# A fused attention and feed-forward kernel: GpSimd and the transfers in program order, one batch turned by TensorE, two kinds of work given to VectorE

## The chip, the cores and the metric

The kernel runs on one core of one Trainium2 chip. The metric is device microseconds of one execution. The engines are named as in the profile: PE is TensorE's matmul stream, PEld its weight load, DVE is VectorE, ACT ScalarE, POOL GpSimd, SP SyncE, whose queue issues most transfers. A line such as L657 is a line of the kernel that ran. PSUM is the memory that TensorE writes to, in banks; the kernel sets three of them aside for attention, as the pool "at".

## The reference, cut to what matters

```python
# q, k, v: (8 batches, 8 heads, 576 tokens, 64), float32; g_norm: (64,)
kv  = einsum('bhsd,bhse->bhde', k, v)
o   = einsum('bhsd,bhde->bhse', q, kv)
rms = sqrt(mean(o * o, axis=-1, keepdims=True) + 1e-06)
x   = (o / rms * g_norm)          # -> 4608 rows of 512
h   = (x @ w1) * (x @ w2) @ w3    # w1, w2: 512 x 1024; w3: 1024 x 1024
out = h @ w_out                   # w_out: 1024 x 512
```

All is float32. The weights arrive in 64 bits and are converted on the chip.

## The kernel before

It folds w3 and w_out into one matrix first (0 to 84 us, the "fold"). Then come nine groups of 512 tokens, which I call T0 to T8: 512 rows of each of the eight batches, and the eight left-over blocks of 64 rows as a ninth. A group is four quarters of "gates" (x w1 times x w2, L569) and a projection (times the folded matrix, L841), both in forms with seven products in place of eight, whose sums VectorE makes. A quarter of gates has four result blocks, finished in the order c12, c22, c11, c21. T0 still converts weights and prepares the folded matrix's sums. T0 to T6 each prepare the next batch's attention besides, in eight steps, two to a quarter. The order of execution is T0 to T6, then the left rows, then the last batch. In the changed kernel the same lines are L615 (gates) and L886 (projection).

A batch's q, and its normalized output, must be turned (transposed) before TensorE can use them. This is done by GpSimd and a transfer:

```python
def turn_by_dma(srcs, apart, turned, dsts):            # (cut)
    nc.gpsimd.tensor_copy(to, words(src) ...)          # L284, L286: split fp32 into two uint16 planes
    yield
    nc.sync.dma_start_transpose(out=turned, in_=apart) # L288
    yield
    nc.gpsimd.tensor_copy(words(dst), src)             # L298: put the planes together
```

The steps of a batch, in the kernel before:

```python
fs[1] += [(a.begin_kv, 2, 3), (a.finish, 0)]     # finish: product and norm of one half
fs[2].append((a.begin_q, 2, 3))                  # turn the other half's q
fs[3].append((a.turn_two, 0))                    # turn the normalized half: this is x
...
fs[5].append((a.finish, 1))
fs[6].append((batch(b + 1).begin_q, 0, 1))       # the NEXT batch's q
fs[6].append((a.turn_two, 1))                    # x, second half
if b % 2:                                        # odd batches: the left rows of two batches
    fs[2].insert(0, (a.q_t_left,))
    fs[4].append((a.product_left,))
    fs[6].append((a.turn_left,))
```

The product takes two of the three "at" banks and its norm reads them:

```python
def product(h):
    o_ps = [bank(ps_at, "at") for _ in range(2)]
    ...                                          # 64 matmuls, L395 (L409 after)
    return norm(o_ps, ...)
def product_left():
    o_ps = [bank(ps_at, "at") for _ in range(2)]
    ...                                          # 32 matmuls, L413 (L427 after)
def norm(o_ps, dsts):
    ...                                          # square (ACT), reduce (DVE), sqrt (ACT), reciprocal (DVE)
    nc.vector.tensor_tensor(out=dsts[i], in0=o_ps[i] ..., in1=inv ..., op=ALU.mult)   # L373 (L387 after)
```

When x is there, VectorE makes the sums of the next group's x: `combine_x`, L611 (L657 after). The gates' own ends are the addition and the product of gates:

```python
nc.vector.tensor_add(c, one, two)                    # L707 (L753 after)
nc.vector.tensor_mul(dst, c[:, 0, :], c[:, 1, :])    # L708 (L754 after)
```

Only TensorE executes in program order (`manual_schedule(engines={PE})`). The order of the instructions on every other engine is set by a scheduler when the kernel is built. Each engine then works through its own list, and an instruction that waits holds up those behind it: in the prediction's lines of T3, VectorE stands 6.37 us at L611 with the gate product L708 behind it.

## Time and profile before

| | us |
|---|---|
| median of three runs | 842.67 (840.91 to 843.88) |
| span of the profiled execution | 840.2 |
| TensorE busy | 779.8 |
| TensorE idle | 60.4 |
| T0 | 110.1 |
| T1, T2, T3, T4, T5, T6 | 82.8, 85.4, 84.8, 85.0, 84.5, 77.5 |
| left rows; last batch with tail | 70.4; 75.6 |

A group begins with its first gate matmul on TensorE's timeline. The left rows show what a group costs with no attention beside it, 70.4 us. The prediction shows the lines of the page that carry this.

### The profile page before, as it was taken

The numbers are of one execution on the slowest core, as the hardware profiler recorded it, in microseconds if no ns is written. First come the engines' busy times: TensorE is split into PE (matmuls) and PEld (weight loads), VectorE is DVE, ScalarE is ACT, GpSimd is POOL, SyncE is SP. The second block draws the span as 40 slices with busy tenths as digits, with TensorE's granted clock in tenths as the row PEclk, the third lists the DMA queues.
The fourth block names the chain that finished last, engine by engine and source line by source line (L and its number), as shares of the span: only waits on it lengthen the run. The fifth ranks groups of instructions, "written<-read, shape, count | busy, mean of one in ns | idle before, by whom it ended". The sixth has DMA issues, their size and how long they took to land.

```text
span 840.2 us, 14371 instructions
## 1 busy us (share of the span) xinstructions
PE 779.8 (93%) x5747; PEld 674.4 (80%) x5747; DVE 537.0 (64%) x1050; ACT 245.7 (29%) x476; POOL 201.4 (24%) x176
## 2 busy tenths in 40 slices
PE   8999786979989998899889997999799999999997
PEld 6455675868879887898789877987798898899897
DVE  7958889923548655754485567554755983575366
ACT  6677431302221322122212221322123222222221
POOL 0016547671340135013301350033003300000000
PEclk9999996999999999899989998999899999999999
DMA  9997663488555747564646564656462263037005
GB/s 323 326 321 217 161 141 78 154 239 293 93 126 192 226 84 158 176 226 95 126 167 226 104 151 147 224 125 126 139 219 51 39 232 127 0 132 226 0 24 184
DMA packets 140166, 134.37 MB, mean 160 GB/s; under 512 B 84036, under 2 KB 128068, under 8 KB 140100
## 3 DMA queue, kind: packets, MB, share of 16 engines
q1 hardware_dynamic: 137648, 118.64, 50.7%
q10 hardware_dynamic: 2452, 14.81, 5.1%
q8 instruction: 45, 0.74, 0.4%
q14 instruction: 21, 0.17, 0.1%
HBM read 100.27 MB, written 16.38 MB: 139 GB/s over the span
## 4 chain that ended last, share of the span: by engine, by line
PE 63%; DMA 10%; DVE 9%; issue 8%; POOL 8%; SPq 1%; ACT 1%; POOLq 0%; DVEq 0%; ACTq 0%
PE mm L569 34%; PE mm L841 19%; PE mm L551 5%; DMA q_sb<-qT 3%; DMA xn<-xT 2%; DMA w3o_sb<-w3o_l 2%; POOL xT L284 1%; PE at L319 1%; POOL w_sb L167 1%; DVE ab L708 1%; PE at L395 1%; DMA w3o_l<-stage 1%; POOL qT L298 1%; DVE xc L611 1%; DVE c L707 1%
## 5 line engine op out<-in xcount | busy, mean ns | idle before, releaser
L569 PE MATMUL mm<-xT,w_sb 128*128 128x256 f32 x768 | 177.0, 380 | 0.0
L569 PEld LDWEIGHTS mm<-xT,w_sb 128*128 128x128 f32 x768 | 146.3, 191 | 20.1 <-issue 0.5
L569 PE MATMUL mm<-xc,ws 128*128 128x256 f32 x576 | 134.1, 386 | 6.1 <-ACT p L582 6.1
L569 PEld LDWEIGHTS mm<-xc,ws 128*128 128x128 f32 x576 | 111.3, 194 | 22.3 <-ACT p L582 6.9
L707 DVE TENSOR_TENSOR c<-mm,u 128x512 f32<-128x512 f32 x36 | 24.8, 689 | 128.0 <-PE mm L569 128.0
L582 ACT COPY u<-mm 128x512 f32<-128x512 f32 x74 | 43.3, 585 | 167.0 <-PE mm L569 137.2
L286 POOL COPY qT<-q_sb 128x1024 uint16<-128x1024 uint16 x28 | 30.9, 1127 | 242.1 <-PE at L395 209.0
L569 PE MATMUL mm<-xc,w_sb 128*128 128x256 f32 x288 | 71.5, 392 | 8.1 <-ACT u L582 8.1
L841 PE MATMUL mm<-w3o_sb,ab 128*128 128x128 f32 x336 | 48.4, 290 | 25.3 <-DVE ab L708 24.5
L582 ACT COPY p<-mm 128x512 f32<-128x512 f32 x74 | 43.1, 585 | 86.9 <-PE mm L569 77.8
L569 PEld LDWEIGHTS mm<-xc,w_sb 128*128 128x128 f32 x288 | 54.6, 194 | 16.8 <-ACT u L582 8.9
L841 PE MATMUL mm<-w3o_sb,raw 128*128 128x128 f32 x500 | 67.0, 288 | 0.4 <-DMA w3o_sb<-w3o_l 0.4
L841 PEld LDWEIGHTS mm<-w3o_sb,ab 128*128 128x128 f32 x336 | 44.6, 205 | 26.5 <-DVE ab L708 25.3
L841 PEld LDWEIGHTS mm<-w3o_sb,raw 128*128 128x128 f32 x500 | 63.6, 204 | 0.8 <-issue 0.6
L569 PE MATMUL mm<-xT,ws 128*128 128x256 f32 x256 | 62.3, 387 | 0.2 <-ACT p L582 0.2
L551 PE MATMUL mm<-chunks,ab 128*128 128x512 f32 x128 | 60.2, 601 | 0.6 <-ACT ab L543 0.6
L708 DVE TENSOR_TENSOR ab<-c 128x256 f32<-128x256 f32 x108 | 56.2, 520 | 2.9
L569 PEld LDWEIGHTS mm<-xT,ws 128*128 128x128 f32 x256 | 49.2, 194 | 7.7 <-ACT p L582 0.6
L167 POOL TENSOR_SCALAR w_sb<-w_sb,g_col 128x1024 f32<-128x1024 f32 x8 | 26.6, 3323 | 82.0 <-ACT kv_sb L330 46.8
L298 POOL COPY xT<-xn 128x1024 uint16<-128x1024 uint16 x28 | 34.1, 1246 | 49.8 <-DMA xn<-xT 49.8
L707 DVE TENSOR_TENSOR c<-p,u 128x512 f32<-128x512 f32 x36 | 27.0, 751 | 29.4 <-ACT u L582 29.1
L298 POOL COPY qT<-q_sb 128x1024 uint16<-128x1024 uint16 x28 | 34.0, 1225 | 31.2 <-DMA q_sb<-qT 31.1
(153 smaller groups left out, 1169.5 us busy)
## 6 DMA issues: line engine op xcount, KB each, us to landing
w3o_sb<-w3o_l SPq DMA_DIRECT2D x26, 896.0 KB, 4.8
raw<-in_moe_w_dram SPq DMA_DIRECT2D x31, 512.0 KB, 7.4
raw<-w3o_l SPq DMA_DIRECT2D x13, 896.0 KB, 4.7
w3o_sb<-w3o_l ACTq DMA_DIRECT2D x11, 896.0 KB, 4.6
k_sb<-in_k_dram SPq DMA_DIRECT2D x32, 256.0 KB, 4.7
v_sb<-in_v_dram SPq DMA_DIRECT2D x32, 256.0 KB, 4.8
q_sb<-in_q_dram SPq DMA_DIRECT2D x32, 256.0 KB, 2.9
out_dram<-raw SPq DMA_DIRECT2D x14, 512.0 KB, 6.1
```

Of the source, the lines that this page charges most:

```text
L167: nc.gpsimd.tensor_scalar(out=dst, in0=dst, scalar1=scale, scalar2=None, op0=ALU.mult)
L284: nc.gpsimd.tensor_copy(to, src.rearrange("p a n w -> p w a n"))
L286: nc.gpsimd.tensor_copy(to, words(src).rearrange("p n w -> p w n"))
L298: nc.gpsimd.tensor_copy(words(dst), src)
L319: nc.tensor.matmul(kv_ps[e * D:(e + 1) * D, r - rs[0], :], lhsT=k_sb[:, e, cols] if j < J else kl[:, 2 * r + e, :], rhs=v_sb[:, e, cols] i ...
L395: nc.tensor.matmul(o_ps[l][tokens, n * D:(n + 1) * D], lhsT=qT[r][rows, e, i, tokens], rhs=kv_b[rows, e, r, :], start=True, stop=True,)
L551: nc.tensor.matmul(sums_ps[half][m], lhsT=w3T[half, c][:, m, :], rhs=chunks[:, c, 1, :], start=(c == 0), stop=(c == KF - 1),)
L569: nc.tensor.matmul(ps[:, u, :], lhsT=lhsT(a_name, u, c), rhs=rhs(b_name, c),  start=(u == 0 and c == 0 and to is None), stop=(c == chunks ...
L582: nc.scalar.copy(t, ps)
L707: nc.vector.tensor_add(c, one, two)
L708: nc.vector.tensor_mul(dst, c[:, 0, :], c[:, 1, :])
L841: nc.tensor.matmul(to[:, i, :], lhsT=x[:, c, :], rhs=y[:, c, :], start=new and place // 4 not in seen, stop=(c == 1), skip_group_check=True,)
```

## The change

The intent is to free TensorE from waits for GpSimd. Four parts:

1. the scaling of the weights by g goes from GpSimd to VectorE;
2. in T0, batch 1's q and x are turned by TensorE with ScalarE copies;
3. the 28 subtractions for the folded matrix's sums go from GpSimd to VectorE, and from T0 into T1's steps;
4. GpSimd and SyncE follow the program's order, the program puts x ahead of q, the last copies of a turn come one step after its begin, and the left product of later odd batches moves from step 4 to step 5.

```diff
-            nc.gpsimd.tensor_scalar(out=dst, in0=dst, scalar1=scale, scalar2=None, op0=ALU.mult)
+            nc.vector.tensor_scalar(out=dst, in0=dst, scalar1=scale, scalar2=None, op0=ALU.mult)
 ...                                              # steps(b)
+        def turn(i, f, *args):                   # copies and transfer in step i, last copies in step i + 1
+            ...
         if b == 1:
+            fs[0] += [(a.begin_kv, 0, 1), (a.begin_q, 0, 1)]
         fs[1] += [(a.begin_kv, 2, 3), (a.finish, 0)]
-        fs[2].append((a.begin_q, 2, 3))
-        fs[3].append((a.turn_two, 0))
+        if b == 1:
+            fs[2] += [(a.q_t_left,), (a.begin_q, 2, 3)]
+            fs[3] += [(a.turn, 0), (a.turn, 1)]
+        else:
+            turn(2, a.x_by_dma, 0)
+            turn(2, a.q_two_by_dma, 2, 3)
+            if odd:
+                turn(3, a.q_left_by_dma)
         ...
         fs[5].append((a.finish, 1))
-        fs[6].append((batch(b + 1).begin_q, 0, 1))
-        fs[6].append((a.turn_two, 1))
-        if b % 2: ...                            # q left 2, product_left 4, turn_left 6
+        if odd:
+            fs[5 if b > 1 else 6].append((a.product_left,))
+        if b == 1:
+            fs[7] += [(a.turn, 2), (a.turn, 3), (a.turn_left,)]
+        else:
+            turn(6, a.x_by_dma, 1)
+            if odd:
+                turn(6, a.x_left_by_dma)
         if more:
+            turn(6 if b > 1 else 7, batch(b + 1).q_two_by_dma, 0, 1)
 ...                                              # prepare_b, now a generator run from T1's steps
-            nc.gpsimd.tensor_sub(t1, b12, b11)   # and three more
+            nc.vector.tensor_sub(t1, b12, b11)   # and three more
 ...
-    ctx.enter_context(tc.manual_schedule(engines={mybir.EngineType.PE}))
+    ctx.enter_context(tc.manual_schedule(
+        engines={mybir.EngineType.PE, mybir.EngineType.Pool, mybir.EngineType.SP}
+    ))
```

More of the change, by code (lines that the diff above doesn't have):

```diff
@@ L298, in turn_by_dma, with together @@
             nc.gpsimd.tensor_copy(words(dst), src)
+    def together(turns):
+        turns = list(turns)
+        while turns:
+            turns = [t for t in turns if next(t, turns) is None]
+            yield
     def attention(b):
@@ L346, in q_by_dma @@
             to = qT[r].rearrange("p e i t -> p (e i t)")
-            all_of(turn_by_dma([q_sb], to, q_sb, [to]))
+            return turn_by_dma([q_sb], to, q_sb, [to])
         st = {}
@@ L352, in q_t_left, with q_left_by_dma @@
             st["qT"] = work.tile([P, NP, P], FP32, name="qT_left", bufs=1)
+            qt_ps = bank(ps_at, "at").rearrange("p (r t) -> p r t", r=NP)
+            for r in range(NP):
+                nc.tensor.transpose(qt_ps[:, r, :], q_left[b // 2][:, 2 * r:2 * r + 2, :], ident)
+            nc.scalar.copy(st["qT"], qt_ps)
+        def q_left_by_dma():
+            st["qT"] = work.tile([P, NP, P], FP32, name="qT_left", bufs=1)
             src = q_left[b // 2].rearrange("p h d -> p (h d)")
             to = st["qT"].rearrange("p r t -> p (r t)")
-            all_of(turn_by_dma([src], to, src, [to]))
+            return turn_by_dma([src], to, src, [to])
         def norm(o_ps, dsts):
@@ L430, in turn, with x_by_dma @@
             nc.scalar.copy(dst, t_ps.rearrange("p (i j) t -> p i (j t)", i=2))
-        def turn_two(h):
+        def x_by_dma(h):
             xn, x = st[h].rearrange("p i l m d -> p (i l) (m d)"), xT[b][:, h]
@@ L437, in turn_two @@
             half = [slice(r * G, (r + 1) * G) for r in range(2)]
-            turns = [
+            return together(
                 turn_by_dma(
@@ L442, in turn_two, with x_left_of, x_left_by_dma @@
                 for r in range(2)
-            ]
-            for _ in range(2):
-                for t in turns:
-                    next(t)
-            for t in turns:
-                all_of(t)
-        def turn_left():
-            n = b // 2
-            x = x_left[:, :, n // 2, :, (n % 2) * P:(n % 2 + 1) * P]
-            xn = st["left"].rearrange("p r e d -> p (r e d)")
+            )
+        def x_left_of():
+            n = b // 2
+            return x_left[:, :, n // 2, :, (n % 2) * P:(n % 2 + 1) * P]
+        def turn_left():
+            t_ps = bank(ps_at, "at").rearrange("p (h r t) -> p h r t", h=2, t=P)
+            for r in range(NP):
+                nc.tensor.transpose(t_ps[:, r // 2, r % 2, :], st["left"][:, r], ident)
+            nc.scalar.copy(x_left_of(), t_ps)
+        def x_left_by_dma():
+            x, xn = x_left_of(), st["left"].rearrange("p r e d -> p (r e d)")
             apart = st["qT"].rearrange("p r t -> p (r t)")
-            all_of(turn_by_dma([xn], apart, xn, [x[:, h] for h in range(2)]))
+            return turn_by_dma([xn], apart, xn, [x[:, h] for h in range(2)])
         def load_ahead(names, r):
@@ L473, in begin_q, with q_two_by_dma, loads @@
             for r in rs:
-                q_by_dma(r)
+                q_t(r)
                 load_ahead("q", r)
+        def q_two_by_dma(*rs):
+            def loads():
+                yield
+                yield
+                for r in rs:
+                    load_ahead("q", r)
+            return together([*(q_by_dma(r) for r in rs), loads()])
         def begin(r):
@@ L480, in begin @@
             load_ahead("q", r)
-        first_done = []
-        def begin_first():
-            if not first_done:
-                first_done.append(begin_q(0, 1))
         def finish(h):
@@ L491, in attention @@
         return SimpleNamespace(**{f.__name__: f for f in (
-            start, begin_kv, begin_q, begin_first, begin, product, finish, turn, turn_two, q_t_left, product_left,
-            turn_left,
+            start, begin_kv, begin_q, begin, product, finish, turn, q_t_left, product_left, turn_left,
+            q_two_by_dma, q_left_by_dma, x_by_dma, x_left_by_dma,
         )})
@@ L508, in steps, with begin @@
         more = b + 1 < B
-        fs = [[] for _ in range(8)]
+        fs, ends = ([[] for _ in range(8)] for _ in range(2))
+        def turn(i, f, *args):
+            t = []
+            def begin():
+                t.append(f(*args))
+                next(t[0])
+                next(t[0])
+            fs[i].append((begin,))
+            if i + 1 < 8:
+                ends[i + 1].append((lambda: all_of(t[0]),))
+            else:
+                to_end.append((lambda: all_of(t[0]),))
+        ends[0] += to_end
+        to_end.clear()
+        odd = b % 2
         if b == 1:
-            fs[0].append((a.begin_kv, 0, 1))
+            fs[0] += [(a.begin_kv, 0, 1), (a.begin_q, 0, 1)]
         fs[1] += [(a.begin_kv, 2, 3), (a.finish, 0)]
-        fs[2].append((a.begin_q, 2, 3))
-        fs[3].append((a.turn_two, 0))
+        if b == 1:
[6 more added lines that the diff above has]
+                turn(3, a.q_left_by_dma)
         if more:
@@ L517, in steps @@
         fs[5].append((a.finish, 1))
-        if more:
-            fs[6].append((batch(b + 1).begin_q, 0, 1))
-        fs[6].append((a.turn_two, 1))
-        if b % 2:
-            fs[2].insert(0, (a.q_t_left,))
-            fs[4].append((a.product_left,))
-            fs[6].append((a.turn_left,))
-            if more:
-                fs[7].append((load_q_left, b + 1))
-        elif more:
-            fs[0].append((load_q_left, b + 1))
-        return iter([lambda s=s: [f(*args) for f, *args in s] for s in fs])
+        if odd:
+            fs[5 if b > 1 else 6].append((a.product_left,))
+        if b == 1:
+            fs[7] += [(a.turn, 2), (a.turn, 3), (a.turn_left,)]
+        else:
+            turn(6, a.x_by_dma, 1)
+            if odd:
+                turn(6, a.x_left_by_dma)
+        if more:
+            turn(6 if b > 1 else 7, batch(b + 1).q_two_by_dma, 0, 1)
+            fs[7 if odd else 0].append((load_q_left, b + 1))
+        return iter([lambda s=e + f: [f(*args) for f, *args in s] for e, f in zip(ends, fs)])
+    to_end = []
     w3T = {}
@@ L744, in b_blocks @@
         return [b[0, 0], t1, t2, b[1, 1], b[0, 1], b[1, 0], t4]
-    def stage_tile():
-        return late_pool.tile([P, 3, 2, P], FP32, name="stage")
     def prepare_b():
@@ L758, in prepare_b @@
             )
-            stage = stage_tile()
-            t1, t2, t4 = (stage[:, i] for i in range(3))
-            nc.gpsimd.tensor_sub(t1, b12, b11)
-            nc.gpsimd.tensor_sub(t2, b22, t1)
-            nc.gpsimd.tensor_sub(b12, b22, b12)
-            nc.gpsimd.tensor_sub(t4, b21, t2)
+            stage = o_sbs[n % 2].rearrange("p m n -> p (m n)")[:, 0:6 * P]
+            t1, t2, t4 = (t.rearrange("p (c n) -> p c n", n=P) for t in (
+                stage[:, i * 2 * P:(i + 1) * 2 * P] for i in range(3)
+            ))
+            nc.vector.tensor_sub(t1, b12, b11)
+            nc.vector.tensor_sub(t2, b22, t1)
+            nc.vector.tensor_sub(b12, b22, b12)
+            nc.vector.tensor_sub(t4, b21, t2)
             nc.sync.dma_start(
@@ L767, in prepare_b @@
             )
-            nc.sync.dma_start(
-                out=w3o_l2[n, :, 1024:PART], in_=stage.rearrange("p i c n -> p (i c n)")
-            )
+            nc.sync.dma_start(out=w3o_l2[n, :, 1024:PART], in_=stage)
+            yield
     loaded_b = []
@@ L942 @@
     w3o_l2 = dram.tile([8, P, PART], FP32, name="w3o_l2")
-    ctx.enter_context(tc.manual_schedule(engines={mybir.EngineType.PE}))
+    ctx.enter_context(tc.manual_schedule(
+        engines={mybir.EngineType.PE, mybir.EngineType.Pool, mybir.EngineType.SP}
+    ))
     fold = fold_cm.__enter__()
@@ L1040, in between @@
             next(pieces, lambda: None)()
+            if T == 1:
+                for _ in range(2):
+                    next(preparing, None)
+                if len(loaded_b) == 0 and next(preparing, 0) == 0:
+                    for _ in range(3):
+                        load_b()
         for p in range(NF):
@@ L1054 @@
                 continue
-            gates(T, p, between if T or p else lambda: batch(1).begin_first())
+            gates(T, p, between if T or p else lambda: None)
             if T == 0:
@@ L1073 @@
         run(combine_x(1))
-        prepare_b()
-        for _ in range(3):
-            load_b()
-        stage = stage_tile()
-        inner_sums.append([stage[:, i] for i in range(3)])
+        preparing = prepare_b()
+        third = late_pool.tile([P, 3, 2, P], FP32, name="inner_sums")
+        inner_sums.append([third[:, i] for i in range(3)])
 _INS = ['q', 'k', 'v', 'g_norm', 'moe_w1', 'moe_w2', 'moe_w3', 'moe_w_out']
```

## The prediction

> **What bounds the kernel now.** The page's first part comes first: TensorE is the fullest engine and everything else has room.
>
> ```profile
> PE 779.8 (93%) x5747; PEld 674.4 (80%) x5747; DVE 537.0 (64%) x1050; ACT 245.7 (29%) x476; POOL 201.4 (24%) x176
> ```
>
> So what can be won is TensorE's idle time, 840.2 - 779.8 = 60 us, plus matmuls that ran slowly. The timeline of TensorE says where it lies. I call the nine token groups T0 to T8: T0 (84 to 194 us) still converts weights; T1 to T6 (194 to 694) each compute one group and prepare the next batch's attention; the last two (694 to 840) only compute. The waits of TensorE:
>
> ```profile
> PE mm L841 <- DVE ab L708: 32.3, 6, 7.3
> PE mm L569 <- ACT u L582: 13.4, 3, 5.3
> PE mm L569 <- ACT p L582: 6.3, 3, 3.4
> ```
>
> The first row is one gap in each of T1 to T6, where a group's gates end and its projection begins: 5.7, 6.4, 7.4, 6.4, 6.0, 0.4 us. The other rows, 19.7 us, are all in T0. Read T3's gap on TensorE, then VectorE before it:
>
> ```profile
> 415.83 0.83 PE L841 MATMUL mm<-raw,ab 128*128 128x128 f32 x6
> 424.02 1.65 PE L841 MATMUL mm<-raw,ab 128*128 128x128 f32 x6 [7.35 <-DVE ab L708]
> ```
>
> ```profile
> 413.20 1.16 DVE L707 TENSOR_TENSOR c<-p,u 128x512 f32<-128x512 f32 x1 [0.29 <-ACT u L582]
> 420.73 0.69 DVE L611 TENSOR_TENSOR xc<-xT,xc 128x512 f32<-128x512 f32 x1 [6.37 <-POOL xT L298]
> ...
> 423.54 0.42 DVE L708 TENSOR_TENSOR ab<-c 128x256 f32<-128x256 f32 x1
> ```
>
> VectorE had the gate TensorE needs (L708) in its queue, behind L611, which combines the NEXT batch's x and waits for GpSimd. GpSimd in turn:
>
> ```profile
> 401.67 2.19 POOL L286 COPY qT<-q_sb 128x1024 uint16<-128x1024 uint16 x2 [11.79 <-issue]
> 409.41 2.25 POOL L298 COPY qT<-q_sb 128x1024 uint16<-128x1024 uint16 x2 [5.55 <-DMA q_sb<-qT]
> 411.60 2.22 POOL L284 COPY xT<-xn 128x1024 uint16<-128x1024 uint16 x2
> 418.45 2.24 POOL L298 COPY xT<-xn 128x1024 uint16<-128x1024 uint16 x2 [4.64 <-DMA xn<-xT]
> ```
>
> x was normalized at 406.43 and left lying to 411.60, while GpSimd finished q, which nobody needs until the next group. In T0 VectorE waits for GpSimd's scaling by g (2.1, 2.7, 1.8 us) and at its end for x:
>
> ```profile
> 94.86 7.10 POOL L167 TENSOR_SCALAR w_sb<-w_sb,g_col 128x1024 f32<-128x1024 f32 x2 [2.99 <-DVE w_sb L165]
> ```
>
> ```profile
> 184.01 1.20 DVE L611 TENSOR_TENSOR xc<-xT,xc 128x512 f32<-128x512 f32 x1 [16.51 <-POOL xT L298]
> ```
>
> **What the Trainium skill says.** "GPSIMD Engine Reference", 3.1: an elementwise tensor_tensor takes GpSimd 1.96 times VectorE's time. Here a 128x256 subtraction takes 0.73 to 0.80 us on GpSimd and 0.41 on VectorE, as stated; the scaling by g is further apart: 2.84 us at best (mean 3.32), against 0.69 for VectorE's tensor_scalar of 128x1024 (L162). "SBUF - State Buffer", Who interferes with whom: a VectorE instruction with two SBUF inputs, or in a two-port mode, and a GpSimd one that reads SBUF block each other. The trace agrees: L622, 128x512, is 0.68 us alone and 1.41 to 1.64 beside GpSimd's copies and scalings. "TensorE: Matmul & The Clock Gate", What's actually happening: an idle window of about 3.4 us halves the clock. The trace agrees after most gaps: at 424.02 six matmuls take 1.65 us, not 0.83, and the next twelve 2.60, not 1.50: about 1.5 us lost behind each gap.
>
> **The change part by part.** The sizes are identical, and TensorE keeps its order of large matmuls; it gains only 40 transposes in T0.
>
> 1. g by VectorE. Eight scalings leave GpSimd (26.6 us there). Three fall before T0, beside a TensorE-bound phase: nothing. Five in T0 cost VectorE 5 x 0.69 = 3.5 us and remove its waits of 6.7 us.
>
> 2. Batch 1 turned by TensorE. It adds 16 (q) + 4 (q left) + 16 (x) + 4 (x left) transposes at about 0.12 us each (eight took 0.95): 4.8 us of TensorE, and ten ScalarE copies of 0.58, 5.8 us on an idle engine. GpSimd's copies leave T0, and with them the chain copy, transfer, copy.
>
> 3. The sums for w3 w_out go from GpSimd in T0 to VectorE in T1: 28 x 0.34 (spacing back to back) = 9.5 us, in a stage in which VectorE is busy 30.7 of 65 us. Their write to memory and the reload lie 20 us ahead of use. Nothing on the path.
>
> T0 added up. GpSimd becomes nearly idle there, so VectorE's doubled instructions shrink: I count about 17 us of stretching between 84 and 187 us. VectorE would do 79.3 - 17 + 3.5 = 66 us of work in T0, against TensorE's 48.3 (gates, as in the last groups) + 24.2 (projection) + 6.7 (attention) + 4.8 = 84. VectorE still leads in the first three quarters of the gates, as each has two conversions of 1.21 + 0.68 + 0.68 + 1.21 + 0.69 = 4.5 us, gates 3.7 and weight sums 2.7, so 15.3 against TensorE's 12.1. Walking VectorE's built order with the undisturbed durations, the first c11 gate (ab at 106.2 before) comes at about 100.5, the second (125) at 117.5, the third (149) at 134; the last quarter starts near 132 in place of 146.4, one 3 us stall left. Then 12.1 + 2 for that quarter, 24.2 + 2.3 for the projection and turns, 1 for small waits: T0 ends near 174, not 194: -20.
>
> 4. x ahead of q. GpSimd and the transfers follow the program. In T3 x's copies begin at 406.5 and end at 408.5; transfer to copy takes 4.8 us (4.6 to 5.0 from L284's end to L298's start); q's first copies fit inside. x is ready at 413.3 + 2.24 = 415.5, not 420.7. What that is worth depends on where VectorE's own order, still the scheduler's, now has L611. In the built kernel:
> - T1: behind the gates. Gap gone: -5.7 - 1.5 = -7.
> - T3, T5: same place. VectorE waits from 413.9 to 415.5, the gate arrives 3.4 us later, 2.2 us of gap stay: -5.1 - 1 and -3.9 - 1, so -6 and -5.
> - T2, T4: two of the L611 that need late x now stand BEFORE the quarter's first gate (c12), not behind it. In T2 x is ready near 330.5; c12's matmuls end at 326.3. The u copy and TensorE's last gate product wait for it: TensorE resumes near 336 in place of 338.4: -2.5 each.
> - T6: its next group uses the left rows, whose product moved from the fifth step to the sixth and whose copies come after x's. Before, it was ready early (gap 0.4). I get xn 660.2, x copied 669.3, left copied 670.8, then c12; the projection resumes near 676 in place of 671: +4.5.
>
> Sum: -20 - 7 - 6 - 5 - 5 + 4.5 = -38.5; 842.67 - 38.5 = 804.
>
> **The rivals.**
> A. VectorE's L611 ahead of c12 takes the place of the wait removed, in T2, T4 and T6. Half of that is already in the sum. Worse, if x's transposes are slowed by k and v loads in flight: q's pair, issued just behind those, took 6.39 us in T3 and 3.24 in T2. Then odd groups gain nothing and T6 loses 7: near 812. Against it: x's transposes come 5 us after those loads were issued.
> B. VectorE becomes the bound of T0: without GpSimd's help its queue could run as long as before. Only 66 of 84 us are its work, but order counts, and TensorE's transposes need PSUM banks that the norm holds. If T0 gains 10 instead of 20: 814.
> C. The transfers in strict order block: a store or a load of the prepared w3 w_out waits in front of k, v or q loads. In T1 a block is written only after a VectorE subtraction scheduled into the third quarter, and loads queue behind it. I see 8 us of slack; if it fails, T1's gain goes: 811.
> D. The scheduler's order proves harmless, x always arrives in time, and all gaps vanish: 20 + 32 + 9 = 61 in place of 38.5: near 782. The built order of T2, T4 and T6 speaks against this.
>
> **Range and chances.** B and A are the likely misses and both make it slower; D's half-way point, and a T0 even shorter, make it faster. Predicted 804, range 794 to 816. Two per cent is 17 us: T0 alone, at -20, passes it, and for "same" both T0 and the x part must fail by half: faster 0.95, same 0.04, slower 0.01.
>
> **What would show it.** Right: T0 ends near 174; no GpSimd row for L167 or the sums; a T1 gap under 1 us; T3 and T5 gaps near 2; T2 and T4 near 4, with VectorE waiting for GpSimd's xT ahead of c12; a new gap of 4 to 5 us in T6; the last two groups unchanged at 70 us each plus the tail. Wrong: T0 over 100 us long (VectorE full, or waits for PSUM); VectorE waits for a store or a w3 w_out write in T1; transfers from x over 6 us; gaps in T3 and T5 as before.

## More of the kernel before

One more view is wanted for what follows, the table by stages: for a stretch of time it gives its length, then the busy time of each engine with its number of instructions, then the granted clock, the share of the transfer engines, and GB/s. This is T0 of the kernel before:

```profile
83.90:194.00 110.10, 90.39 (x617) 75.40 (x616) 81.48 (x119) 27.25 (x54) 67.30 (x55) 0.91 0.59 155
```

GpSimd, the fifth engine, works 67.3 us here, more than in any other group, and VectorE works 81.5 of 110 us.

## The result, and the profile after

The changed kernel takes 808.83 us (median of four runs, 807.72 to 811.43) against 841.79 for the kernel before on the same chip (840.78 to 843.88). The ratio is 0.961, with a 95% interval of 0.9577 to 0.9642. Here and below, a ratio is the mean time of one kernel's fast runs over that of the other's of the same rounds, so it is not quite the ratio of the medians. The prediction was 804.0, range 794 to 816.

The first part of the page, after:

```profile
PE 773.9 (96%) x5787; PEld 670.7 (83%) x5787; DVE 543.6 (67%) x1086; ACT 251.5 (31%) x486; POOL 130.7 (16%) x119
```

TensorE's idle time fell from 60.4 to 806.1 - 773.9 = 32.2 us. Its busy time fell by 5.9 us although it does 40 more transposes, and fewer matmuls fall into the slow stretches behind a wait: the mean granted clock rose from 0.970 to 0.984. The waits of TensorE after (releaser: total, count, longest):

```profile
PE mm L886 <- DVE ab L754: 11.8, 5, 5.6
PE at L427 <- DVE xn L387: 10.4, 3, 4.1
```

The first row is the wait at the projection, 32.3 us before. The second is new. The two rows of T0 in the prediction's fence, 19.7 us, have gone. By stage, from the two profiled executions:

| | before | after | change | predicted |
|---|---|---|---|---|
| fold | 83.9 | 84.5 | +0.6 | 0 |
| T0 | 110.1 | 85.3 | -24.8 | -20 |
| T1 | 82.8 | 78.2 | -4.6 | -7 |
| T2 | 85.4 | 82.5 | -2.9 | -2.5 |
| T3 | 84.8 | 82.8 | -2.0 | -6 |
| T4 | 85.0 | 82.5 | -2.5 | -2.5 |
| T5 | 84.5 | 82.6 | -1.9 | -5 |
| T6 | 77.5 | 82.0 | +4.5 | +4.5 |
| left rows | 70.4 | 70.4 | 0 | 0 |
| last batch | 75.6 | 75.4 | -0.2 | 0 |
| sum | 840.2 | 806.1 | -34.1 | -38.5 |

(The rows are rounded singly, the sum is that of the spans.)

T0 first. The same row as above, of the changed kernel:

```profile
84.50:169.80 85.30, 84.85 (x657) 74.06 (x656) 64.94 (x125) 32.74 (x64) 2.06 (x2) 1.00 0.28 83
```

TensorE is busy 84.85 of 85.3 us, at full clock: T0 is bound by TensorE and nothing else. VectorE has 64.9 us of work (66 were predicted). What the scaling by g costs on each engine is in the table of groups (busy, mean ns of one, idle before), of before and then of after:

```profile
L167 POOL TENSOR_SCALAR w_sb<-w_sb,g_col 128x1024 f32<-128x1024 f32 x8 | 26.6, 3323 | 82.0 <-ACT kv_sb L330 46.8
```

```profile
L167 DVE TENSOR_SCALAR w_sb<-w_sb,g_col 128x1024 f32<-128x1024 f32 x8 | 6.0, 748 | 0.1
```

Then T3, where the prediction fell short. The timeline of GpSimd, VectorE and TensorE around the end of T3's gates, after:

```profile
381.97 2.24 POOL L298 COPY xT<-xn 128x1024 uint16<-128x1024 uint16 x2 [2.86 <-DMA xn<-xT]
383.99 0.83 PE L886 MATMUL mm<-raw,ab 128*128 128x128 f32 x6
...
384.25 0.69 DVE L657 TENSOR_TENSOR xc<-xT,xc 128x512 f32<-128x512 f32 x1 [2.21 <-POOL xT L298]
384.63 2.60 POOL L298 COPY qT<-q_sb 128x1024 uint16<-128x1024 uint16 x2 [0.42 <-DMA q_sb<-qT]
384.86 1.37 DVE L754 TENSOR_TENSOR ab<-c 128x256 f32<-128x256 f32 x1
386.15 1.63 DVE L657 TENSOR_TENSOR xT<-xT 128x512 f32<-128x512 f32 x1
...
388.97 0.41 DVE L754 TENSOR_TENSOR ab<-c 128x256 f32<-128x256 f32 x1
...
389.44 1.65 PE L886 MATMUL mm<-raw,ab 128*128 128x128 f32 x6 [4.62 <-DVE ab L754]
```

x arrives at 384.21, 0.2 us after TensorE began the projection's first six matmuls; the prediction had it 0.3 us before. But directly behind x's last copies GpSimd makes q's, and beside them the gate product L754 takes 1.37 us, not 0.42, and the x sum L657 takes 1.63, not 0.69. The two together lose 1.9 us. From x's arrival to the end of the awaited L754 pass 5.2 us. The gap is 4.62, and the six matmuls after it still run at half speed (1.65 us, not 0.83).

T5 has the same stretching, and there x is late as well. GpSimd and VectorE in T5, after:

```profile
548.31 2.24 POOL L298 COPY xT<-xn 128x1024 uint16<-128x1024 uint16 x2 [3.89 <-DMA xn<-xT]
550.49 2.71 POOL L298 COPY qT<-q_sb 128x1024 uint16<-128x1024 uint16 x2
550.58 1.60 DVE L657 TENSOR_TENSOR xc<-xT,xc 128x512 f32<-128x512 f32 x1 [3.23 <-POOL xT L298]
552.11 1.37 DVE L754 TENSOR_TENSOR ab<-c 128x256 f32<-128x256 f32 x1
```

From the end of x's first copies to the start of its last ones pass 5.9 us, not the 4.8 of T3, so that x is there at 550.55, 1.25 us after the projection's first matmuls began at 549.30. L657 and L754 lose 1.9 us here too, and the gap is 5.61.

Then T2, where the size was right. TensorE and VectorE at the left product:

```profile
286.52 1.16 PE L409 MATMUL at<-kv_sb,qT 64*64 64x64 f32 x64
287.81 0.29 PE L427 MATMUL at<-kv_sb,qT_left 64*64 64x64 f32 x2
...
291.30 0.69 PE L427 MATMUL at<-kv_sb,qT_left 64*64 64x64 f32 x30 [3.19 <-DVE xn L387]
291.92 3.42 PE L615 MATMUL mm<-xc,w_sb 128*128 128x256 f32 x8
```

The left product now comes right behind the product. Its first matmuls go to the one free bank, and then it waits until the norm (L387) has read the product's banks. The eight gate matmuls behind it take 3.42 us, not 1.99. The same stands in T4 (3.19 us) and T6 (4.05). These three waits are the new row of 10.4 us.

### The profile page after: what moved, and what is told of

Its sections match the earlier page's. It is cut to its first block, busy times and chain, and to the rows that moved or that the text cites. A ratio compares the mean times of both kernels' runs of the same rounds, so it can differ in the third digit from the quotient of the medians.

```text
span 806.1 us, 14409 instructions
## 1 busy us (share of the span) xinstructions
PE 773.9 (96%) x5787; PEld 670.7 (83%) x5787; DVE 543.6 (67%) x1086; ACT 251.5 (31%) x486; POOL 130.7 (16%) x119
## 4 chain that ended last, share of the span: by engine, by line
PE 75%; DMA 9%; issue 5%; DVE 4%; POOL 4%; SPq 1%; ACT 1%; DVEq 0%; POOLq 0%; ACTq 0%
PE mm L615 43%; PE mm L886 21%; PE mm L597 6%; DMA xn<-xT 3%; PE at L326 2%; POOL xT L298 2%; DMA raw<-in_moe_w_dram 2%; PE at L409 1%; DMA v_sb<-in_v_dram 1%; DVE c L753 1%; POOL xT L284 1%; DMA raw<-in_moe_w_out_dram 1%; DVE ab L754 1%; DMA k_sb<-in_k_dram 1%; PE at L584 1%
## 5 line engine op out<-in xcount | busy, mean ns | idle before, releaser
L615 PE MATMUL mm<-xc,ws 128*128 128x256 f32 x576 | 130.2, 379 | 0.0
L615 PEld LDWEIGHTS mm<-xc,ws 128*128 128x128 f32 x576 | 109.4, 190 | 14.9
L753 DVE TENSOR_TENSOR c<-mm,u 128x512 f32<-128x512 f32 x36 | 24.8, 690 | 112.8 <-PE mm L615 112.8
L628 ACT COPY u<-mm 128x512 f32<-128x512 f32 x74 | 43.3, 585 | 147.4 <-PE mm L615 143.0
L615 PE MATMUL mm<-xc,w_sb 128*128 128x256 f32 x288 | 73.6, 401 | 0.0
L284 POOL COPY xT<-xn 128x1024 uint16<-128x1024 uint16 x24 | 26.0, 1113 | 278.8 <-DVE xn L387 278.8
L886 PE MATMUL mm<-w3o_sb,raw 128*128 128x128 f32 x500 | 64.5, 279 | 0.3 <-DMA w3o_sb<-w3o_l 0.3
L886 PEld LDWEIGHTS mm<-w3o_sb,raw 128*128 128x128 f32 x500 | 60.5, 195 | 1.6 <-issue 0.5
L754 DVE TENSOR_TENSOR ab<-c 128x256 f32<-128x256 f32 x108 | 55.5, 514 | 2.9
L886 PE MATMUL mm<-w3o_sb,ab 128*128 128x128 f32 x336 | 45.6, 279 | 7.5 <-DVE ab L754 7.1
L886 PEld LDWEIGHTS mm<-w3o_sb,ab 128*128 128x128 f32 x336 | 41.9, 194 | 8.7 <-DVE ab L754 7.9
L286 POOL COPY qT<-q_sb 128x1024 uint16<-128x1024 uint16 x24 | 25.4, 1086 | 142.8 <-PE at L409 139.1
L753 DVE TENSOR_TENSOR c<-p,u 128x512 f32<-128x512 f32 x36 | 26.8, 744 | 31.7 <-ACT u L628 31.5
L597 PEld LDWEIGHTS mm<-chunks,ab 128*128 128x128 f32 x128 | 21.9, 190 | 23.2 <-issue 15.8
L897 ACT COPY u<-mm 128x512 f32<-128x512 f32 x23 | 13.5, 586 | 85.1 <-DVE raw L910 46.2
```

Source lines behind the costliest of these rows:

```text
L284: nc.gpsimd.tensor_copy(to, src.rearrange("p a n w -> p w a n"))
L286: nc.gpsimd.tensor_copy(to, words(src).rearrange("p n w -> p w n"))
L597: nc.tensor.matmul(sums_ps[half][m], lhsT=w3T[half, c][:, m, :], rhs=chunks[:, c, 1, :], start=(c == 0), stop=(c == KF - 1),)
L615: nc.tensor.matmul(ps[:, u, :], lhsT=lhsT(a_name, u, c), rhs=rhs(b_name, c),  start=(u == 0 and c == 0 and to is None), stop=(c == chunks ...
L628: nc.scalar.copy(t, ps)
L886: nc.tensor.matmul(to[:, i, :], lhsT=x[:, c, :], rhs=y[:, c, :], start=new and place // 4 not in seen, stop=(c == 1), skip_group_check=True,)
```

## The experiments

Twelve kernels ran, all correct. In each, the kernel before ran on the same chip, with medians of 841.3 to 842.5. The changed kernel was not in these rounds, so that a difference to it is no surer than the 1.2 us between these medians. My theory after the first reading had four parts. (a) T0's gain is the sum of the three pieces of work that left GpSimd. (b) In T3 and T5 it is VectorE's order, with GpSimd's copies of q beside it, that holds TensorE. (c) In T2, T4 and T6 it is the PSUM banks. (d) The program order of GpSimd and the transfers is what brings x early. The rivals were that one of the pieces carries T0 alone; that x's own arrival bounds T2 to T6, as the prediction has it; and that the order does nothing.

The lengths of stages below are those of the one profiled execution of each kernel. Where T1 is over 83 us, TensorE stood there for loads (e2, e3, e2c, e12: 4 to 8 us), for q (e5), or at the projection as in the kernel before (e7).

| kernel | median us | ratio to before | T0 | T1 | T2 | T3 | T4 | T5 | T6 |
|---|---|---|---|---|---|---|---|---|---|
| changed kernel | 808.83 | 0.961 | 85.3 | 78.2 | 82.5 | 82.8 | 82.5 | 82.6 | 82.0 |
| e4_g_gpsimd | 818.27 | 0.971 | 94.7 | 78.6 | 82.4 | 81.9 | 82.9 | 84.0 | 81.3 |
| e7_before_g (from before) | 830.89 | 0.9862 | 98.8 | 84.8 | 85.5 | 83.1 | 85.0 | 84.3 | 76.9 |
| e5_sums_gpsimd | 818.81 | 0.9708 | 85.3 | 87.5 | 82.6 | 82.2 | 83.0 | 84.8 | 81.6 |
| e6_b1_dma | 814.6 | 0.9683 | 90.5 | 81.4 | 82.7 | 81.7 | 82.5 | 83.1 | 81.4 |
| e9_auto_order | 823.48 | 0.9765 | 84.6 | 81.8 | 85.8 | 85.2 | 88.4 | 83.2 | 82.2 |
| e3_dve_order | 801.5 | 0.9526 | 84.5 | 89.1 | 81.4 | 78.1 | 81.8 | 78.1 | 81.9 |
| e1b_left_step6 | 807.21 | 0.9583 | 84.7 | 79.6 | 83.0 | 82.3 | 83.9 | 83.6 | 77.6 |
| e8_order_and_left | 797.95 | 0.948 | 86.9 | 81.4 | 81.0 | 78.1 | 82.6 | 80.6 | 77.1 |
| e2_q_step7 | 815.04 | 0.966 | 84.6 | 84.4 | 82.5 | 84.7 | 82.4 | 86.0 | 81.4 |
| e2c_q_tensor | 811.5 | 0.9627 | 85.1 | 85.2 | 82.8 | 81.7 | 82.5 | 80.6 | 81.3 |
| e11_order_left4 | 793.95 | 0.9425 | 84.6 | 79.5 | 79.0 | 78.1 | 82.2 | 78.8 | 76.6 |
| e12_order_left4_q | 796.44 | 0.9455 | 84.9 | 83.4 | 83.4 | 78.8 | 82.6 | 77.1 | 76.1 |

### What T0 gained from: e4, e7, e6, e5

The changed kernel with the scaling back on GpSimd:

```diff
-            nc.vector.tensor_scalar(out=dst, in0=dst, scalar1=scale, scalar2=None, op0=ALU.mult)
+            nc.gpsimd.tensor_scalar(out=dst, in0=dst, scalar1=scale, scalar2=None, op0=ALU.mult)
```

> The changed kernel with the eight scalings by g back on GpSimd. Theory (T0 is set by VectorE's conversions, and GpSimd's scalings both delay it and stretch its instructions): five scalings of 2.8 to 3.8 us return in T0, VectorE waits for each again (2 to 3 us), T0 goes from 85 to 91 to 96 us, total 814 to 820. Rival (T0 was set by the other copies and sums on GpSimd, not by g): T0 within 2 us of 85.

T0 took 94.7 us, 9.4 more, and the waits of the second row of T0 came back. TensorE's timeline of this kernel:

```profile
125.77 3.78 PE L615 MATMUL mm<-xc,ws 128*128 128x256 f32 x8 [4.53 <-ACT p L628]
```

The reverse, the kernel before with this part of the change alone:

```diff
-            nc.gpsimd.tensor_scalar(out=dst, in0=dst, scalar1=scale, scalar2=None, op0=ALU.mult)
+            nc.vector.tensor_scalar(out=dst, in0=dst, scalar1=scale, scalar2=None, op0=ALU.mult)
```

> The kernel before, with only the scalings by g moved to VectorE. Theory: the three waits of 2.1, 2.7 and 1.8 us and the stretching beside the scalings go, T0 falls from 110 to 100 to 104 us; T1 to T6 unchanged; total 832 to 836. If g is all that matters in T0: near 820. If the sums and copies on GpSimd set T0: near 841.

T0 took 98.8 us, 11.3 less than before, and no other stage moved by more than 2 us. So the scaling by g, eight instructions, is worth 9 to 11 of the 25 us of T0, whichever side it is tried from; the median of 830.89 is 1 us below what I had expected.

The changed kernel with batch 1 turned by GpSimd and transfers, as the other batches are:

```diff
-            fs[0] += [(a.begin_kv, 0, 1), (a.begin_q, 0, 1)]
+            fs[0] += [(a.begin_kv, 0, 1)]          # its first q as before, in T0's first quarter
-            fs[2] += [(a.q_t_left,), (a.begin_q, 2, 3)]
-            fs[3] += [(a.turn, 0), (a.turn, 1)]
+            turn(2, a.x_by_dma, 0)
+            turn(2, a.q_two_by_dma, 2, 3)
+            turn(3, a.q_left_by_dma)
-            fs[7] += [(a.turn, 2), (a.turn, 3), (a.turn_left,)]
+            turn(6, a.x_by_dma, 1)
+            turn(6, a.x_left_by_dma)
```

> The changed kernel with batch 1 turned by GpSimd copies and transposing transfers as before the change (in program order, x ahead of q). TensorE loses 40 transposes, 4.8 us by my estimate. Theory (the turns on TensorE buy VectorE an undisturbed T0): the 28 copies come back into T0 and stretch VectorE, T0 is 88 to 95 us, not 85, with waits of TensorE on it, total 811 to 818. Rival (TensorE was not waiting in T0, so the transposes are pure cost once g and the sums are gone): T0 near 81, total near 804.

T0 became 5.2 us longer and T1 3.2 us, the latter because batch 2's q was late on GpSimd (waits of 1.43 and 0.60 us at T1's product). In T0 of the changed kernel TensorE is busy 5.4 us with the 40 added transposes and waits 0.45 us in all, so turning a batch on the fullest engine still paid: without them it waited instead (2.76, 1.96 and 1.28 us in T0 of this run).

The changed kernel with the 28 subtractions on GpSimd, still in T1's steps:

```diff
-            nc.vector.tensor_sub(t1, b12, b11)     # and the three others
+            nc.gpsimd.tensor_sub(t1, b12, b11)     # and the three others
```

> The changed kernel with the 28 subtractions for w3 w_out on GpSimd again, but in program order, in T1. Theory (where they lie, T1, counts more than who does them): GpSimd needs 28 x 0.75 = 21 us in T1, of 54 us of gates; T1 grows by at most 3 us through x's copies queueing behind them; total 808 to 812. Rival (GpSimd's place in the order makes x late and VectorE is stretched): T1 longer by 5 us or more, total 814 or more.

T1 took 87.5 us, 9.3 more. The timeline of TensorE and GpSimd in T1 of this kernel:

```profile
210.64 2.63 POOL L298 COPY xT<-xn 128x1024 uint16<-128x1024 uint16 x2
213.22 2.24 POOL L298 COPY qT<-q_sb 128x1024 uint16<-128x1024 uint16 x2
...
214.42 2.23 PE L409 MATMUL at<-kv_sb,qT 64*64 64x64 f32 x64 [4.73 <-POOL qT L298]
```

GpSimd, in strict order now, gets to q's copies late, and TensorE waits for q: its last two subtractions ahead of these copies stood 4.49 us for a write of the sums to memory. Here I had thought the subtractions harmless on GpSimd; they are not, and the rival holds. In a strict order, what is put in front of the wanted copy delays it.

Taken away one at a time from the changed kernel, g, batch 1 and the sums cost 9.4, 5.8 and 10.0 us of the median. They add up to 25.2, but that this is close to T0's 24.8 is no proof of part (a): the 10.0 of the sums lies in T1 (T0 stayed at 85.3), where the change had put them. In T0 itself g and batch 1 account for 9.4 + 5.2 = 14.6 us. The other 10 are not shown by a run of their own; no kernel puts the subtractions back into T0.

### What the order is worth: e9

The changed kernel with GpSimd and the transfers left to the scheduler again:

```diff
-        engines={mybir.EngineType.PE, mybir.EngineType.Pool, mybir.EngineType.SP}
+        engines={mybir.EngineType.PE}
```

> The changed kernel with GpSimd and the transfers left to the scheduler again, all else as changed. Theory (the program order is what brings x early): in T3 and T5 q's copies come ahead of x's again and TensorE waits for the combining of x by 5 us or more, T1 4 to 5 us longer since VectorE's order turns there too; total 815 to 825. Rival (the order of GpSimd and the transfers is worth nothing, as T2 to T5 are bounded by VectorE's order and PSUM): total 807 to 811.

The median is 823.48: the order is worth 14.7 us. In T3 TensorE waits longer again, and in T2 VectorE's sums of x stand ahead of the gate that TensorE needs. TensorE in T3, then VectorE and TensorE in T2:

```profile
398.16 1.65 PE L886 MATMUL mm<-raw,ab 128*128 128x128 f32 x6 [6.93 <-DVE ab L754]
```

```profile
308.05 1.12 DVE L657 TENSOR_TENSOR xc<-xT,xc 128x512 f32<-128x512 f32 x1 [5.37 <-POOL xT L298]
309.09 1.15 DVE L657 TENSOR_TENSOR xT<-xT 128x512 f32<-128x512 f32 x1
310.16 0.68 DVE L753 TENSOR_TENSOR c<-mm,u 128x512 f32<-128x512 f32 x1
```

```profile
311.57 3.55 PE L615 MATMUL mm<-xc,w_sb 128*128 128x256 f32 x8 [2.71 <-ACT u L628]
```

The x sum waits 5.37 us for GpSimd while the gate addition L753 lies behind it; ScalarE's copy, and TensorE with it, wait for that addition. In T4 the same wait is 5.0 us. This is the wait that the prediction expected in T2 and T4 of the changed kernel; it needs x to be late, which here it is.

### VectorE's order and the PSUM banks: e3, e1b, e8, e11

The changed kernel with VectorE in program order too, in each group's last quarter of gates and its projection:

```diff
+                with tc.manual_schedule(engines={mybir.EngineType.DVE}):
                     gates(T, p, between, lambda name: all_of(f() for f in following[name]))
 ...
+            with tc.manual_schedule(engines={mybir.EngineType.DVE}):
                 project_twice(T, last, [] if last else combine_x(groups[n + 1]))
```

> The changed kernel, with VectorE held to the program's order in each group's last gate quarter and its projection, so that all four steps that combine the next x (L657) stand behind the gates; left product and PSUM use as in the changed kernel. Theory (VectorE's order causes T3 and T5, PSUM banks cause T2, T4 and T6): the gaps of 4.6 and 5.6 us ahead of the projections of T3 and T5 go under 1 us, T3 and T5 shorten from 82.7 to about 77 us each; T2, T4 and T6 keep the waits of 3.2, 3.2 and 4.1 us at the left product and stay within 1 us of 82.5, 82.5 and 82. Total near 797 to 799. Rival (the prediction's own: T2, T4 and T6 are long because combining x stands ahead of the first gate): these three fall by 2 us or more each as well, total under 793. Second rival (strict order makes VectorE late elsewhere): projections slow down, total 806 or more.

T3 and T5 fell from 82.8 and 82.6 to 78.1 each. T2, T4 and T6 stayed at 81.4, 81.8 and 81.9, and TensorE's waits for the banks stayed at 3.19, 3.19 and 4.05 us. VectorE and TensorE in T3:

```profile
394.73 0.66 DVE L754 TENSOR_TENSOR ab<-c 128x256 f32<-128x256 f32 x1
...
395.45 0.94 PE L886 MATMUL mm<-raw,ab 128*128 128x128 f32 x6 [1.16 <-DVE ab L754]
```

No sum of x stands ahead of the awaited gate any more, and the gap is 1.16 us. GpSimd copies x and q beside it as before (L754 and its neighbours took up to 1.26 us). So what the two odd stages lose is the order on VectorE: x on time is of no use to a queue that puts its sums ahead of the gate. T1 was slow in this profiled execution: TensorE waited 5.87 and 2.56 us for loads of the prepared matrix. Whether the edit does this or only this execution is not shown; it was the slowest of the four (808.54; the others 799.11, 800.05 and 802.96).

The changed kernel with the left product one step later:

```diff
-            fs[5 if b > 1 else 6].append((a.product_left,))
+            fs[6].append((a.product_left,))
```

> The changed kernel, with the left rows' product one step later (step 6 in place of 5) in batches 3, 5 and 7, when the norm has given its PSUM banks back. VectorE's order, which the scheduler chooses, changes with it in T2, T4 and T6 (the late x steps now stand behind the gates in T2, T4 and T6). PSUM theory: no wait at the left product, no half-speed matmuls behind it; T2 and T4 go from 82.5 to about 77, T6 from 82 to 73 to 75; T3 and T5 stay near 82.7; total near 790. Rival (late x is the bound, the PSUM wait only hides it): the waits move to the start of the projection, T2, T4 and T6 stay within 2 us of their length, total 804 or more.

The waits for the banks are gone, and T6 is 4.4 us shorter. But T2 and T4 are not, and the total of 807.21 is where the rival had it (804 or more): TensorE came earlier to the projection and waited there. TensorE in T2, and in T4:

```profile
306.19 1.65 PE L886 MATMUL mm<-w3o_sb,ab 128*128 128x128 f32 x6 [2.44 <-DVE ab L754]
```

```profile
471.51 0.94 PE L886 MATMUL mm<-w3o_sb,ab 128*128 128x128 f32 x6 [2.44 <-DVE ab L754]
```

It is not the rival's cause, though. VectorE and GpSimd ahead of the first of these gaps:

```profile
301.61 1.14 DVE L754 TENSOR_TENSOR ab<-c 128x256 f32<-128x256 f32 x1
302.42 2.63 POOL L298 COPY xT<-xn 128x1024 uint16<-128x1024 uint16 x2
302.78 1.26 DVE L667 TENSOR_TENSOR raw<-ab,ab 128x256 f32<-128x256 f32 x1
...
305.26 0.88 DVE L754 TENSOR_TENSOR ab<-c 128x256 f32<-128x256 f32 x1
```

VectorE does not wait for x, and no sum of x stands ahead of the awaited gate: the scheduler's order changed with the edit. VectorE runs without a pause from 300.6 us on, with the left product's norm ahead of these gates and GpSimd's copies beside them, and five instructions up to the awaited gate take 2.7 us more than undisturbed, about the length of the gap. That this stretching is the cause in T2 and T4 is read from the trace; no run takes it alone away.

Both edits together:

> Both edits together: VectorE in program order around the projections, the left product at step 6. If the two causes are separate, the gains add: T2 to T5 at 77 each, T6 near 73 to 75, total near 779. If both are one and the same delay of x, the total is no better than the better of the two runs alone.

The median is 797.95, not 779, the profiled execution being the slowest with 802.34. T6 is 77.1 and T3 78.1, but T2 and T4 are still 81.0 and 82.6: at step 6 the left product's norm falls among the last gates on VectorE, and its copies among the subtractions ahead of the projection. So neither of the two places behind the product that were tried is good. The next kernel puts it ahead, at step 4 where it had been before the change, with its q turned a step earlier, and keeps VectorE's order:

```diff
                 # and VectorE's program order, as in the first kernel of this section
-                turn(3, a.q_left_by_dma)
+                turn(2, a.q_left_by_dma)
-            fs[5 if b > 1 else 6].append((a.product_left,))
+            fs[4 if b > 1 else 6].append((a.product_left,))
-                turn(6, a.x_left_by_dma)
+                turn(5, a.x_left_by_dma)
```

> VectorE in program order around the last gate quarter and the projection, and the left product back at step 4, its q turned at step 2 and its x at step 5. Theory (two causes in series in T2, T4, T6: TensorE's wait for the PSUM banks that the norm of the product still holds when the left product comes in the next step after it, and then VectorE's order ahead of the projection): no wait of 3 to 4 us at the left product, T2 and T4 about 78, T6 73 to 76, T3 and T5 78 as with the order alone, total 783 to 792. Rival (the left q, turned one step earlier, is late or its copies stretch VectorE elsewhere): TensorE waits for it at step 4 by 2 us or more, T2, T4 and T6 above 80, total 796 to 803.

The median is 793.95 (792.01 to 796.34), ratio 0.9425 to the kernel before, 14.9 us below the changed kernel and 2 us above the range I had expected. No wait for banks is left, and the left q was at most 0.17 us late. T2 is 79.0, T3 78.1, T5 78.8, T6 76.6. T4 alone is at 82.2, against my 78. GpSimd, VectorE and TensorE at its projection:

```profile
461.46 2.54 POOL L298 COPY xT<-xn 128x1024 uint16<-128x1024 uint16 x2 [2.75 <-DMA xn<-xT]
461.73 1.26 DVE L845 TENSOR_TENSOR raw<-raw,ab 128x256 f32<-128x256 f32 x1
463.02 1.26 DVE L846 TENSOR_TENSOR raw<-ab,raw 128x256 f32<-128x256 f32 x1
463.95 2.63 POOL L298 COPY qT<-q_sb 128x1024 uint16<-128x1024 uint16 x2
464.21 1.37 DVE L668 TENSOR_TENSOR raw<-raw,ab 128x256 f32<-128x256 f32 x1
465.50 1.37 DVE L668 TENSOR_TENSOR ab<-ab 128x256 f32<-128x256 f32 x1
...
467.26 1.23 PE L886 MATMUL mm<-w3o_sb,ab 128*128 128x128 f32 x4 [2.21 <-DVE ab L848]
```

The four copies of x and q fall, one after the other, on four subtractions ahead of the one that TensorE awaits, and each takes 1.3 to 1.4 us instead of 0.42. In T2 of the same kernel they fell a little otherwise. Which subtractions are hit depends on when the transposing transfer lands, and I have no experiment that sets that.

### q behind x: e2, e2c, e12

Two tries to take q's copies away from x's, for part (b). In the first, the next batch's q begins a step later in the stages concerned:

```diff
-            turn(6 if b > 1 else 7, batch(b + 1).q_two_by_dma, 0, 1)
+            turn(6 if b > 1 and odd else 7, batch(b + 1).q_two_by_dma, 0, 1)
```

> The changed kernel, with the next batch's first q turned one step later (step 7) in even batches, so that GpSimd's q copies no longer follow x's directly. Theory (in T3 and T5, beyond x's arrival, q's last copies stretch VectorE's L657 and L754 from 0.68 and 0.42 to 1.4 to 1.6 us just when the gate is awaited): the stretched pair goes, the gaps of T3 and T5 shrink from 4.6 and 5.6 to about 2.5 to 3.5, total 803 to 806. Rival (only x's arrival matters): no change within 0.3 per cent, near 809; if x itself comes earlier without q's copies between, it shows as an earlier last x copy.

It failed, and in an instructive way: T3 and T5 became longer (84.7 and 86.0). GpSimd and VectorE in T3:

```profile
389.23 2.48 POOL L286 COPY qT<-q_sb 128x1024 uint16<-128x1024 uint16 x2
389.32 1.49 DVE L657 TENSOR_TENSOR xc<-xT,xc 128x512 f32<-128x512 f32 x1 [2.13 <-POOL xT L298]
...
390.73 1.25 DVE L754 TENSOR_TENSOR ab<-c 128x256 f32<-128x256 f32 x1
```

Now it is q's first copies (L286) that come directly behind x's last, and stretch a sum of x and a gate product again; its last copies fall on the projection's subtractions and cost another wait of 0.94 us. The gaps are 4.29 and 5.33 us. A later place in the program is not a later time: nothing else stood in GpSimd's list, and q's copies began as x's ended, at 389.2. Of the median's 6 us, T1 has a part that is not this: in the profiled execution TensorE waited 4.62 us there for a load.

In the second, q of those batches is turned by TensorE:

```diff
-            turn(6 if b > 1 else 7, batch(b + 1).q_two_by_dma, 0, 1)
+            if b % 2 == 0:
+                fs[6].append((batch(b + 1).begin_q, 0, 1))
+            else:
+                turn(6 if b > 1 else 7, batch(b + 1).q_two_by_dma, 0, 1)
```

> The changed kernel with the next batch's q, in the even batches, turned by TensorE with ScalarE's copies at step 6, instead of by GpSimd's copies and a transfer. Theory (in T3 and T5 it is GpSimd's copies of q, directly behind those of x, that stretch VectorE's combining of x to 1.6 us and the c12 subtraction to 1.37): the subtraction and the combining ahead of the projection go back to about 0.42 and 0.68 us, the gaps of 4.62 and 5.61 us at the projection of T3 and T5 shrink to 2.5 to 3.3, the stages end 1 to 3 us earlier although TensorE gains about 1 us of turns each; total 804 to 807. Rival (x's own arrival bounds those stages and the stretch doesn't matter): gaps unchanged, stages longer by the turns, total 809 to 811.

VectorE in T3, and TensorE there:

```profile
392.83 0.69 DVE L660 TENSOR_TENSOR xc<-xT,xc 128x512 f32<-128x512 f32 x1 [4.14 <-POOL xT L298]
...
394.04 0.69 DVE L660 TENSOR_TENSOR xT<-xT 128x512 f32<-128x512 f32 x1
394.64 0.42 DVE L757 TENSOR_TENSOR ab<-c 128x256 f32<-128x256 f32 x1
```

```profile
396.84 1.65 PE L889 MATMUL mm<-raw,ab 128*128 128x128 f32 x6 [3.56 <-DVE ab L757]
```

(Lines are three further down in this kernel.) The stretching is gone, 0.69 and 0.42 us, and the gaps fall from 4.62 to 3.56 in T3 and from 5.61 to 2.42 in T5; the stages from 82.8 and 82.6 to 81.7 and 80.6. These falls of 1.1 and 3.2 us are not a clean measure of the copies: the scheduler now puts a gate addition (L756) between the sums of x, which costs 0.6 us, and in T5 x comes 0.8 us before the projection's first matmuls, not 1.25 after them. The durations give the stretching as 1.9 us in each stage, above. The first kernel of the section before, with the copies where they were and only VectorE's order mended, shows the order to be what exposes TensorE to it. The median did not gain (811.5, against 804 to 807 expected) because the edit has a fault: in T1 the load of that q had not landed at step 6, and TensorE waited 5.10 us for it, so that T1 took 85.2.

```profile
221.92 1.94 PE L345 MATMUL at<-ident,q_sb 128*128 128x128 f32 x8 [5.10 <-DMA q_sb<-in_q_dram]
```

Last, the best kernel with this edit added:

> The previous kernel with the next batch's q, in the even batches, turned by TensorE as well. Theory: with VectorE's order mended the copies of q no longer delay what the projection needs, so that turning q on TensorE only adds its turns, about 1 us in each of T3 and T5: total 0 to 3 us above the previous one. Rival (the copies still cost something behind x): T3 and T5 fall to 77 or less and the total by 1 to 3 us.

The median is 796.44, 2.5 us above the best one, within what the theory allowed. The same fault is in it (4.16 us in T1), and T2 had the copies fall on its subtractions as T4 had above (83.4). The two medians lie within each other's run-to-run spread of about 4 us, so I do not decide between them on this.

## Why the prediction was right, point by point, and where it was not

The time is 808.83 against 804.0, inside the range, and it is faster by over 2%, as was given a chance of 0.95. The sum of the steps was 38.5 us, and 34.1 came in the profiled execution.

- **T0, -20: right in kind, mis-sized; -24.8 came.** VectorE's work was foreseen well (66 us against 64.9), TensorE's too (84 against 84.85). The term that failed is the walk through VectorE's order, with the third c11 gate at 134 and "one 3 us stall left". VectorE finished that gate at 129.1 and TensorE never waited more than 0.26 us. The walk had the three gates at 100.5, 117.5 and 134; they came at 98.5, 113.8 and 129.1. The prediction's own count of 15.3 us a quarter is what the trace shows (15.3 and 15.4 us between these); the walk had put 17 and 16.5.
- **T1, -7: right in kind; -4.6 came.** The gap fell from 5.72 to 0.57 us, as predicted under 1. The gates take the same 53.6 us as before, so all that is missing lies in the projection, and its matmuls add up to it: the gap that stays (0.57), about 0.5 us in the 18 matmuls behind it, two waits of 0.33 and 0.36 us for loads of the prepared matrix, and 0.7 us in the matmuls around these.
- **T3 and T5, -6 and -5: most of it missing; -2.0 and -1.9 came.** The step that failed is "the gate arrives 3.4 us later, 2.2 us of gap stay": the gaps are 4.62 and 5.61. What the prediction did not count is that GpSimd's copies of q, put behind x by the change itself, run beside just those VectorE instructions. The 3.4 us became 5.2 in T3 and 5.1 in T5. The prediction had quoted this very contention for T0 and then walked T3 with undisturbed durations. The rest is x itself: against the place that the prediction gave it in T3 and took over for T5, it came 0.5 us later in T3 and 1.6 us in T5, where its transfer took 5.9 us and not 4.8. With these two terms the gaps come out to within 0.1 us. That sums of x stand ahead of the gate at all, the prediction had right: with that order mended, both stages fell to 78.1.
- **T2, T4, T6, -2.5, -2.5 and +4.5: right to half a microsecond, and for the wrong reason.** The step that failed is the wait. The prediction expected TensorE to stand for x ahead of the gate c12, and in T6 for late left rows. VectorE did wait there (1.04 us in T2, 4.03 in T6), but TensorE hardly did (0.31 and 0.64 us at the projections of T2 and T4, none in T6). It had stood before that at the moved left product for PSUM banks, 3.19, 3.19 and 4.05 us, and lost 1.4 to 2.9 us more in the slow matmuls behind it. Moving the product away from the norm took the wait away and gave T6 back 4.4 us. In T2 and T4 it gave back nothing, as other work took its place. Whether the predicted wait would have held TensorE in the changed kernel without the one for the banks, no run shows. The agreement of the sizes was chance.
- **The last two groups, 0: right,** 70.4 and 75.4 against 70.4 and 75.6.
- **The rivals.** A came in part: VectorE's waits ahead of c12 are there, behind the banks, and x's transfer was slow in T5. B did not come; its remark on PSUM banks was the right thought in the wrong stage. C: loads of the prepared matrix did come late in T1, by 0.7 us in the profiled execution and by over 8 us in that of the kernel with VectorE's order alone, so the slack there is thinner than the 8 us I had seen. D did not come.
- **Sums and readings that were off.** A as described, with nothing gained in T3 and T5 and 7 us lost in T6, makes 817.5 by the prediction's own figures, not 812. Both parts failing by half would still leave 19 us, more than the 17 of 2%. VectorE's work in the first 65 us of T1 is 34.6 us in the trace, not 30.7. None of these carries the result.

What stays open: what the subtractions cost in T0; what holds T2 and T4 once the banks are free, beyond the reading of the trace; why GpSimd's copies hit the awaited subtractions in T4 of the best kernel and less so in T2, and how much T1 varies with the loads from one execution to the next; each kernel has one trace.

## What to carry to other kernels

Moving work off a slow engine can pay twice, for the time on that engine and for the neighbour whose instructions it was holding up, but an instruction put "behind" the wanted one still runs beside its consumer, so look at what each copy will lie next to. When a step of the program is moved, count the buffers that its new neighbour holds: two products of two banks each do not fit three banks. And when a size agrees, ask the trace whether the cause does too; a wait that is taken away can leave the stage as long as it was, because other work moves into its place.

## What the Trainium skill lacked or had wrong

- "GPSIMD Engine Reference", 3.1, gives one ratio of GpSimd to VectorE, 1.96 for tensor_tensor. A tensor_scalar by a column of 128x1024 float32 took 3.32 us against 0.75 (mean of eight each): 4.4 times, and 3.8 for GpSimd's fastest, 2.84 us. The page has no ratio for it.
- "SBUF — State Buffer", Who interferes with whom, calls the shared port pair an exclusive lock. The runs agree, and add the size for a run of GpSimd copies of about 1.3 us each: each hits another VectorE instruction with two SBUF inputs, so 0.42 us became 1.26 to 1.37 four times in a row. The page gives no such case.
- "TensorE: Matmul & The Clock Gate", What's actually happening, gives one idle window of about 3.4 us as what slows the clock. Here six matmuls ran at half speed (1.65 us, not 0.83; granted clock 0.50) after an idle time of only 2.44 us in T2 of e1b_left_step6, so a shorter gap can be enough; after the same 2.44 us in its T4 six took 0.94 us, at a granted clock of 1.00. That eight ran at full speed (1.99) after 3.65 us in T0 of the kernel before does not contradict the page, which calls the window free-running.
